# A softmax in four pieces between score tiles, and two fewer, larger weight and cache transfers, in a one-core decode block

## The chip, the cores and the metric

The kernel runs on one core of a Trainium2 chip. The metric is device microseconds (us) for one execution. Three executions took 187.05, 187.17 and 187.21 us, so the median is 187.17 us. One further execution was profiled; it took 187.01 us.

Engines are named as in the profile: PE is the matrix engine and PEld its weight load, DVE the vector engine, ACT the scalar engine, POOL the general engine, SP the engine that issues the DMAs. SPq is SP's instruction queue.

## What is computed

Two sequences with one new token each pass a transformer block: adaLN modulation, attention over a window of the cache, then a GELU-gated feed-forward part. Everything in memory is bf16.

```python
mod = (silu(c) @ w_mod)              # 640 -> 6*640: sa, ca, ga, sb, cb, gb
h = layernorm(x) * (1 + ca) + sa
q = (h @ wq)                          # 640 -> 32 heads * 192
k, v = k_cache[:, :, 3072:4096], v_cache[:, :, 3072:4096]   # W = 1024 keys
p = softmax(q . k * 192 ** -0.5)
x = x + ga * ((p . v) @ wo)           # 6144 -> 640
h = layernorm(x) * (1 + cb) + sb
x = x + gb * ((gelu(h @ w_gate) * (h @ w_up)) @ w_down)     # F = 1536
```

K and V of the window are 2 x 32 x 1024 x 192 values each, 25.2 MB each. With wq and wo (7.9 MB each), w_mod (4.9 MB) and the three feed-forward weights (2.0 MB each) one execution reads 76.9 MB.

## The kernel before

**The cache.** A partition holds a quarter of one head's window: 32 heads x 4 quarters = 128 partitions, 256 keys each. For each row b (0 or 1) these 256 keys are cut into four tiles of 64 (`NTL = 4`, `J = 64`), a tile is 3 MiB. Tiles lie in slots: slots 0 to 3 are the tensor `ring`, slots 4 and 5 the front of `r1` (shown as r), which holds wq first and wo last. `items` (L336) lists the cache loads in their order: tile pairs in one transfer of 6 MiB each, except V's last two tiles of row 1, which are two transfers of 3 MiB. I write K0a for row 0's tiles 0 and 1, K0b for its tiles 2 and 3, and V0a to V1b alike. `load_kv(n)` issues the items up to the n-th.

**The order.** A small scheduler (`_Sched`) keeps one list of operations for each engine, in the order in which the code calls `S.op` and `S.dma`; an engine works through its list in order and waits on semaphores for what it reads and overwrites. So where a call stands in the code sets its place in each queue. All DMAs are issued by SP, in the order: w_mod, c, x, wq, the cache items, wo, w_gate, w_up, w_down, out. A cache load waits until the last reader of its slots has ended: V0a for the K0b tiles' reductions, V0b for row 1's second tile, V1a for row 1's fourth tile, V1b for the two products of V0a (`PV0_0`, `PV0_1`). wo, which overwrites wq and slots 4 and 5, waits for `PV0_2` and `PV0_3`; the feed-forward weights wait for `PV1_0` and `PV1_1`.

**Scores.** `scores` (L554) goes through half tiles: `d_mul` (L465) multiplies half a K tile by q in place on DVE, `filler` gives PE four matmuls without a use (they hold its clock), `p_reduce` (L476) sums 12 slices on PE into a PSUM bank, and `d_rows` (L483) ends the sum of the half tile before on DVE.

**Softmax.** `softmax(b)` is a chain of nine short operations: `pmax` and `T` (maximum for each partition, then a PE transpose), `max`, `gx` and `Bc` (maximum for each head, scaled, then spread by a PE matmul), `nb` and `exp` (copy of the bias on DVE, exponential on ACT), `den` and `rden` (a PE matmul sums the denominators, DVE inverts). Both chains stand after the last score tile.

**Values.** `weighted` alternates `d_mask` (L511, DVE builds the masked probabilities `Em`, two buffers) and `p_pv` (L523, 32 matmuls on PE for one tile). `normalize` scales row 0's sums, then row 1's four tiles follow, then `p_sel` puts the heads in place and `oT` (L597) transposes in three parts.

**After attention.** wo comes in four transfers of 16, 16, 12 and 4 of its 48 tiles; the products are four groups on PE, each waiting for its transfer (L628). `warm(n, ...)` gives PE n idle matmuls after a group (`WO_WARM`). Then come the second layer norm, the gate product (L646, then 8 idle matmuls), the up product, the gate-up product on DVE (L660), a transpose, the down product in three parts (L669) and two DVE operations (L676, L678) before the output's DMA.

Of the kernel before, what the change touches and what calls it, by code (L numbers as in the profile page):

```python
# [5 lines left out]
ALU = mybir.AluOpType  # L6
ACTF = mybir.ActivationFunctionType
AX = mybir.AxisListType
# [95 lines left out]
def bass_adaLN_cond__sliding_block_cached__geglu_ffn__decode_kernel(  # L104
# [15 lines left out]
    P = 128  # L120
    B, _, D = A_x.shape
    _, H, Sk, Dh = A_k_cache.shape
# [13 lines left out]
    QP = P // H  # L136
# [10 lines left out]
    SCALE = float(Dh) ** -0.5  # L147
# [6 lines left out]
    NS = 4  # L154
    SL = J * Dh
    WQ_SPLIT = [5]
    assert sum(WQ_SPLIT) == KT
    WO_SPLIT = [16, 16, 12, 4]
    OT_SPLIT = [16, 16, 16]
    assert sum(WO_SPLIT) == NT and sum(OT_SPLIT) == NT  # L160
    WU_SPLIT = [5]
# [2 lines left out]
    assert sum(WD_SPLIT) == FT  # L164
    ND = 4

    WO_WARM = [0, 8, 0, 9]
    WU_WARM = [5]
    WD_WARM = [5, 0, 0]

# [1 line left out]
    with es:  # L172
        S = _Sched(nc, es)
# [38 lines left out]
        ident_f = sb("ident_f", [P, P], F32)  # L212
        one = sb("one", [1, 1], F32)
# [5 lines left out]
        DS = sb("DS", [P, P], F32)  # L219
# [16 lines left out]
        S_sb = Sg[:, :].rearrange("p (b k) -> p b k", b=2)  # L236
        gl = Sg[:, 0:FN]
        ones_f = Sg[:, 0:P]
        M1 = sb("M1", [P, 1], F32)
        gm = sb("gm", [1, H], F32)  # L240
        gx = sb("gx", [1, H, QP], F32)
        nb = sb("nb", [P, 1], F32)
        E_sb = sb("E_sb", [P, 2, KP], BF16)
        Em = sb("Em", [P, 2, J, H], BF16)
        esum = sb("esum", [P, 2], F32)
        rden = sb("rden", [P, 2], F32)
        On = sb("On", [P, 2, Dh], BF16)
        ps = es.enter_context(nc.psum_tensor("ps", [P, 8, 512], F32))

        BK_T = 2  # L250
# [8 lines left out]
        def bank(k):  # L259
            return ("bank", k)  # L260
# [6 lines left out]
        sem_wg = S.sem("d_wg")  # L267
        sem_wu = [S.sem("d_wu%d" % i) for i in range(len(WU_SPLIT))]
        sem_wd = [S.sem("d_wd%d" % i) for i in range(len(WD_SPLIT))]
        sem_ring = [S.sem("d_ring%d" % i) for i in range(4)]  # L270
        sem_out = S.sem("d_out")

        def k_dma(dst, src):
# [6 lines left out]
        def dram_rows(v):  # L280
# [9 lines left out]
             reads=[("S", 0, 0, 0), ("S", 0, 0, 1), ("S", 0, 1, 0), ("S", 0, 1, 1)], writes=["ident_f"], name="ident_f")  # L290
        S.op("pool", lambda e: e.tensor_copy(out=ident_b[:, :], in_=ident_f[:, :]),
             reads=["ident_f"], writes=["ident_b"], name="ident_b")
# [3 lines left out]
             reads=["ident_f"], writes=["G32"], name="G32")  # L296
        S.op("dve", lambda e: e.tensor_reduce(out=M32[:, :], in_=ident_f[:, :].rearrange("p (h t) -> p h t", t=QP), axis=AX.X, op=ALU.add),
             reads=["ident_f"], writes=["M32"], name="M32")
        S.op("dve", lambda e: e.tensor_copy(out=M32b[:, :], in_=M32[:, :]), reads=["M32"], writes=["M32b"], name="M32b")
        S.op("dve", lambda e: e.tensor_copy(out=Bsel[:, :].rearrange("p (a m) -> p a m", m=SQ),  # L300
                                            in_=G32[:, :].unsqueeze(1).broadcast_to([P, NJ, SQ])),
             reads=["G32"], writes=["Bsel"], name="Bsel")

        S.op("dve", lambda e: e.tensor_copy(out=DS[:, :].rearrange("p (a m) -> p a m", m=SQ),
                                            in_=M32[:, :].unsqueeze(1).broadcast_to([P, NJ, SQ])),
# [17 lines left out]
        def ring_keys(slot):  # L323
# [10 lines left out]


        items = [("k", 0, 0, 2, 0, 0), ("k", 0, 2, 2, 2, 1), ("k", 1, 0, 2, NS, 2), ("k", 1, 2, 2, 0, 0), ("v", 0, 0, 2, 2, 1),  # L336
                 ("v", 0, 2, 2, NS, 2), ("v", 1, 0, 2, 0, 0), ("v", 1, 2, 1, 2, 1), ("v", 1, 3, 1, 3, 3)]
        place = {(kind, b, t0 + i): slot + i for kind, b, t0, nt, slot, _ in items for i in range(nt)}
        assert NTL == 4 and len(place) == 4 * NTL

# [3 lines left out]
        def load_kv(upto, deps=()):  # L344
            while keep["kv"] < upto:
                kind, b, t0, nt, slot, sm = items[keep["kv"]]
                cache = A_v_cache if kind == "v" else A_k_cache
                S.dma("sp", k_dma(tile_f(slot, nt),
                                  cache[b, :, K0:Sk, :].rearrange("h (q r) d -> h q r d", q=QP)[:, :, J * t0:J * (t0 + nt), :].rearrange("h q r d -> h q (r d)")),
                      sem_ring[sm], writes=[k for i in range(nt) for k in ring_keys(slot + i)], deps=deps, name="ld_%s%d_%d" % (kind, b, t0))  # L350
                keep["kv"] += 1
# [108 lines left out]
        def filler(n=1):  # L460
            warm(n * ND, BK_W)
# [19 lines left out]
        def d_rows(b, t, hf):  # L481
            a = J * t + JH * hf
            S.op("dve", lambda e: e.tensor_reduce(out=S_sb[:, b, a:a + JH], in_=ps[:, hf, 0:JH * GC].rearrange("p (j c) -> p j c", j=JH),  # L483
                                                  axis=AX.X, op=ALU.add),
                 reads=[bank(hf)], writes=[("S", b, t, hf)], name="rows%d_%d_%d" % (b, t, hf))

        def softmax(b):
            sk = [("S", b, t, hf) for t in range(NTL) for hf in range(2)]
            S.op("dve", lambda e: e.tensor_reduce(out=M1[:, :], in_=S_sb[:, b, :], axis=AX.X, op=ALU.max),
                 reads=sk, writes=["M1"], name="pmax%d" % b)  # L490
            S.op("pe", lambda e: e.transpose(ps[0:1, BK_T, 0:P], M1[:, :], ident_f[:, :]),  # L491
                 reads=["M1", "ident_f"], writes=[bank(BK_T)], name="T%d" % b)
            S.op("dve", lambda e: e.tensor_reduce(out=gm[:, :], in_=ps[0:1, BK_T, 0:P].rearrange("k (h t) -> k h t", t=QP), axis=AX.X, op=ALU.max),
                 reads=[bank(BK_T)], writes=["gm"], name="max%d" % b)
            S.op("dve", lambda e: e.tensor_scalar(out=gx[:, :, :], in0=gm[:, :].unsqueeze(2).broadcast_to([1, H, QP]),
                                                  scalar1=-SCALE, scalar2=None, op0=ALU.mult),
                 reads=["gm"], writes=["gx"], name="gx%d" % b)
            S.op("pe", lambda e: e.matmul(ps[:, BK_T, P:P + 1], lhsT=gx[:, :, :].rearrange("k h t -> k (h t)"), rhs=one[:, :],  # L498
                                          start=True, stop=True),
                 reads=["gx", "one"], writes=[bank(BK_T)], name="Bc%d" % b)  # L500
            S.op("dve", lambda e: e.tensor_copy(out=nb[:, :], in_=ps[:, BK_T, P:P + 1]), reads=[bank(BK_T)], writes=["nb"], name="nb%d" % b)  # L501
            S.op("act", lambda e: e.activation(out=E_sb[:, b, :], in_=S_sb[:, b, :], func=ACTF.Exp, scale=SCALE, bias=nb[:, 0:1], accum_out=esum[:, b:b + 1]),  # L502
                 reads=sk + ["nb"], writes=[("E", b), ("esum", b)], name="exp%d" % b)
            S.op("pe", lambda e: e.matmul(ps[:, BK_T, P + 2:P + 3], lhsT=DS[:, :], rhs=esum[:, b:b + 1], start=True, stop=True),  # L504
                 reads=[("esum", b), "DS"], writes=[bank(BK_T)], name="den%d" % b)
            S.op("dve", lambda e: e.reciprocal(out=rden[:, b:b + 1], in_=ps[:, BK_T, P + 2:P + 3]),
                 reads=[bank(BK_T)], writes=[("rden", b)], name="rden%d" % b)


        def d_mask(b, t):  # L510
            S.op("dve", lambda e: e.tensor_tensor(out=Em[:, t % 2, :, :], in0=E_sb[:, b, J * t:J * (t + 1)].unsqueeze(2).broadcast_to([P, J, H]),  # L511
                                                  in1=M32b[:, :].unsqueeze(1).broadcast_to([P, J, H]), op=ALU.mult),
                 reads=[("E", b), "M32b"], writes=[("Em", t % 2)], name="mask%d_%d" % (b, t))

        def p_pv(b, t):
            vs = slot_of("v", b, t)
            n = J // 2

            def f(e):
                last = None  # L520
                for jp in range(n):
                    r = 2 * SQ * (jp % 2)
                    last = e.matmul(ps[r:r + 2 * H, BK_O, 0:ON],  # L523
                                    lhsT=Em[:, t % 2, 2 * jp:2 * jp + 2, :].rearrange("p j c -> p (j c)"),
                                    rhs=tile_v(vs)[:, 2 * jp:2 * jp + 2, :],
                                    start=(t == 0 and jp < 2), stop=(t == NTL - 1 and jp >= n - 2), tile_position=(0, r), skip_group_check=True)
                return last
            keep[("pv", b, t)] = S.op("pe", f, reads=[("Em", t % 2)] + ring_keys(vs), writes=[bank(BK_O)], name="PV%d_%d" % (b, t))
# [22 lines left out]
            S.op("pe", f, reads=["SEL"] + [("On", b, g) for g in range(NJ)], writes=[bank(BK_H + c) for c in range(NQC)], name="sel%d" % b)  # L551


        def scores(b, ta, tb):  # L554
            for t in range(ta, tb):
                for hf in range(2):
                    d_mul(b, t, hf)
                    filler()
                    p_reduce(b, t, hf)
                    if (b, t, hf) != (0, 0, 0):  # L560
                        d_rows(*((b, t, 0) if hf else (b, t - 1, 1) if t else (b - 1, NTL - 1, 1)))

        def weighted(b, ta, tb):
            for t in range(ta, tb):
                d_mask(b, t)
                p_pv(b, t)
# [2 lines left out]
        load_kv(4)  # L569
        scores(0, 2, 4)  # L570
        load_kv(5)
        scores(1, 0, 2)
        load_kv(6)
        scores(1, 2, 4)
        load_kv(7)
        d_rows(1, NTL - 1, 1)
        softmax(0)
        softmax(1)
        weighted(0, 0, 2)
        load_kv(9)  # L580
        weighted(0, 2, 4)
        normalize(0)
        for t in range(NTL):
            d_mask(1, t)
            p_pv(1, t)
            if t == NTL - 1:
                p_sel(0)
        normalize(1)
# [127 lines left out]
```

## Time and profile before

| what | value |
|---|---|
| median of three executions | 187.17 us |
| profiled execution, its own time | 187.01 us |
| its span, first to last instruction | 185.7 us |
| busy: PE, DVE, ACT | 117.2, 106.6, 13.9 us |
| DMA queue q1: data, share of 16 engines' span | 76.88 MB, 96.7% |
| mean granted PE clock | 0.915 |
| chain that ended last, by engine | DMA 43%, DVE 36%, PE 16% |

The chain that ended last is found backwards from the last instruction, from each step to what released it. It passes through several engines because transfers wait for buffers that the engines free. A transfer's time "to landing" runs from its issue to its completion, so it holds the time that it stood behind other transfers. Every landing time in the prediction is the issue plus that time, both from the DMA view, or the start of the instruction that waited for it.

### The profile page before, as it was taken

How to read it: one execution, taken by the hardware profiler on the slowest of the kernel's cores; microseconds unless marked ns; L12 is line 12 of the kernel's file. 1: busy time of each engine (PE TensorE's matmuls, PEld its weight loads, DVE VectorE, ACT ScalarE, POOL GpSimd, SP SyncE). 2: the span in 40 equal slices, each digit the busy share in tenths (PEclk: the TensorE clock that was granted, in tenths of full speed). 3: DMA queues.
4: the chain of work that ended last, by engine and by line, in shares of the span. 5: the costliest groups of instructions: out<-in, count | busy, mean ns of one | idle time of the engine just before them, and what ended most of it. 6: DMA issues, size and time to landing. Idle time of an engine off the chain costs nothing.

```text
span 185.7 us, 2254 instructions
## 1 busy us (share of the span) xinstructions
PE 117.2 (63%) x1014; PEld 60.8 (33%) x1014; DVE 106.6 (57%) x114; ACT 13.9 (7%) x24; POOL 4.9 (3%) x12
## 2 busy tenths in 40 slices
PE   0004500871079899988999885349928977299844
PEld 0001200440024334433344342226614654265422
DVE  6801600020598999999999993294556714803331
ACT  2001400013000000000000000200010004100400
POOL 8200000000000000000000000000000000000000
PEclk9999999998559999999999999558996999859999
DMA  7999998898999989899999989899999999999991
GB/s 248 414 437 477 463 463 389 371 491 371 487 413 434 468 381 459 381 487 402 455 424 434 459 381 466 381 487 413 395 434 424 424 435 424 413 408 435 422 392 50
DMA packets 2925, 77.02 MB, mean 415 GB/s; under 512 B 356, under 2 KB 356, under 8 KB 868
## 3 DMA queue, kind: packets, MB, share of 16 engines
q1 hardware_dynamic: 2916, 76.88, 96.7%
q8 instruction: 8, 0.13, 0.3%
q14 instruction: 1, 0.01, 0.0%
HBM read 76.88 MB, written 0.00 MB: 414 GB/s over the span
## 4 chain that ended last, share of the span: by engine, by line
DMA 43%; DVE 36%; PE 16%; SPq 1%; ACT 1%; issue 1%; POOL 1%; DVEq 0%; POOLq 0%
DMA ring<-in_A_k_cache_dram 24%; DVE ring L465 19%; DMA ring<-in_B_w_down_dram 18%; PE ps L523 10%; DVE r L465 7%; DVE Sg L483 5%; PE ps L476 4%; DVE Em L511 2%; SPq L274 1%; ACT E_sb L502 1%; PE ps L504 1%; PE ps L498 1%; DVE On L540 0%; ACT On L536 0%; PE ps L491 0%
## 5 line engine op out<-in xcount | busy, mean ns | idle before, releaser
L465 DVE TENSOR_TENSOR ring<-ring,qbc 128x6144 bf16<-128x6144 bf16 x12 | 40.1, 3351 | 8.4 <-DMA ring<-in_A_k_cache_dram 8.4
L476 PE MATMUL ps<-ring,ident_b 128*128 128x512 bf16 x144 | 34.7, 393 | 13.0 <-DVE ring L465 13.0
L454 PE MATMUL ps<-qbc,ident_b 128*128 128x384 bf16 x120 | 24.7, 339 | 0.7 <-ACT qbc L432 0.7
L523 PE MATMUL ps<-ring,Em 128*64 128x384 bf16 x192 | 19.6, 371 | 7.8 <-DVE Em L511 6.6
L476 PEld LDWEIGHTS ps<-ring,ident_b 128*128 128x128 bf16 x144 | 13.6, 100 | 32.7 <-DVE ring L465 17.2
L511 DVE TENSOR_TENSOR Em<-E_sb,M32b 128x2048 bf16<-128x2048 bf16 x8 | 18.1, 2288 | 5.5 <-PE ps L523 5.5
L523 PEld LDWEIGHTS ps<-ring,Em 128*64 128x64 bf16 x192 | 12.4, 125 | 14.6 <-DVE Em L511 7.3
L454 PEld LDWEIGHTS ps<-qbc,ident_b 128*128 128x128 bf16 x120 | 11.6, 101 | 10.9 <-issue 2.8
L401 PE MATMUL ps<-ring,scT 128*32 128x480 bf16 x40 | 4.4, 601 | 16.0 <-DVE scT L358 16.0
L465 DVE TENSOR_TENSOR r<-r,qbc 128x6144 bf16<-128x6144 bf16 x4 | 13.4, 3352 | 0.0
L483 DVE TENSOR_REDUCE Sg<-ps 128x32 f32<-128x512 f32 x16 | 11.0, 687 | 3.4 <-PE ps L476 3.4
L424 PE MATMUL ps<-r,hT 128*32 128x384 bf16 x80 | 5.8, 475 | 10.7 <-DMA r<-in_A_wq_dram 10.7
L476 PE MATMUL ps<-r,ident_b 128*128 128x512 bf16 x48 | 11.1, 380 | 1.8 <-DVE r L465 1.8
L434 DVE CAST aux<-ps 128x384 bf16<-128x384 f32 x4 | 2.0, 553 | 16.6 <-PE ps L424 15.7
L628 PE MATMUL ps<-r,aux 128*32 128x160 bf16 x192 | 5.1, 271 | 4.4 <-DMA r<-in_A_wo_dram 2.6
L424 PEld LDWEIGHTS ps<-r,hT 128*32 128x32 bf16 x80 | 3.2, 135 | 13.8 <-issue 11.6
L476 PEld LDWEIGHTS ps<-r,ident_b 128*128 128x128 bf16 x48 | 4.4, 98 | 8.1 <-DVE r L465 3.4
L401 PEld LDWEIGHTS ps<-ring,scT 128*32 128x32 bf16 x40 | 1.2, 132 | 17.5 <-DVE scT L358 16.0
L540 DVE TENSOR_SCALAR On<-ps,rden 32x192 bf16<-32x192 f32 x4 | 1.7, 418 | 8.9 <-ACT On L536 8.9
L502 ACT ACTIVATE E_sb<-Sg,nb 128x256 bf16<-128x256 f32 x2 | 1.0, 507 | 75.6 <-DVE nb L501 75.6
L628 PEld LDWEIGHTS ps<-r,aux 128*32 128x32 bf16 x192 | 4.3, 114 | 5.8 <-DMA r<-in_A_wo_dram 3.6
L523 PE MATMUL ps<-r,Em 128*64 128x384 bf16 x64 | 5.4, 327 | 0.0
(73 smaller groups left out, 65.6 us busy)
## 6 DMA issues: line engine op xcount, KB each, us to landing
ring<-in_A_k_cache_dram SPq DMA_DIRECT2D x3, 6144.0 KB, 40.3
ring<-in_A_v_cache_dram SPq DMA_DIRECT2D x2, 6144.0 KB, 23.3
r<-in_A_wq_dram SPq DMA_DIRECT2D x1, 7680.0 KB, 30.7
r<-in_A_k_cache_dram SPq DMA_DIRECT2D x1, 6144.0 KB, 38.4
r<-in_A_v_cache_dram SPq DMA_DIRECT2D x1, 6144.0 KB, 23.3
ring<-in_A_v_cache_dram SPq DMA_DIRECT2D x2, 3072.0 KB, 17.6
r<-in_A_wo_dram SPq DMA_DIRECT2D x2, 2560.0 KB, 23.7
ring<-in_w_mod_dram SPq DMA_DIRECT2D x1, 4800.0 KB, 14.2
```

The costliest lines, as they stand in the source:

```text
L274: return lambda e: e.dma_start(dst, src)
L401: last = e.matmul(ps[SQ * j:SQ * j + SQ, bk, 0:3 * DN].rearrange("p (i n) -> p i n", i=3), lhsT=scT[:, k, :], rhs=wm_v[:, k, 3 * part * D: ...
L424: last = e.matmul(ps[SQ * j:SQ * j + SQ, BK_H + c, 0:QC], lhsT=hT[:, k, :], rhs=wq_v[:, k, RN * j + QC * c:RN * j + QC * (c + 1)], start=( ...
L434: S.op("dve", lambda e: e.tensor_copy(out=dst, in_=src), reads=reads, writes=writes, name=name)
L454: last = e.matmul(ps[:, bk, 0:2 * Dh], lhsT=ident_b[:, :], rhs=qbc[:, :, :].rearrange("p b d -> p (b d)"), start=True, stop=True)
L465: S.op("dve", lambda e: e.tensor_tensor(out=tile_v(ks)[:, hf * JH:(hf + 1) * JH, :], in0=tile_v(ks)[:, hf * JH:(hf + 1) * JH, :], in1=qbc[ ...
L476: last = e.matmul(o_ap, lhsT=ident_b[:, :], rhs=tile_v(ks)[:, hf * JH:(hf + 1) * JH, ci * GC:(ci + 1) * GC], start=(ci == 0), stop=(ci == ...
L483: S.op("dve", lambda e: e.tensor_reduce(out=S_sb[:, b, a:a + JH], in_=ps[:, hf, 0:JH * GC].rearrange("p (j c) -> p j c", j=JH), axis=AX.X, ...
L502: S.op("act", lambda e: e.activation(out=E_sb[:, b, :], in_=S_sb[:, b, :], func=ACTF.Exp, scale=SCALE, bias=nb[:, 0:1], accum_out=esum[:, ...
L511: S.op("dve", lambda e: e.tensor_tensor(out=Em[:, t % 2, :, :], in0=E_sb[:, b, J * t:J * (t + 1)].unsqueeze(2).broadcast_to([P, J, H]), in ...
L523: last = e.matmul(ps[r:r + 2 * H, BK_O, 0:ON], lhsT=Em[:, t % 2, 2 * jp:2 * jp + 2, :].rearrange("p j c -> p (j c)"), rhs=tile_v(vs)[:, 2 ...
L628: last = e.matmul(ps[SQ * j:SQ * j + SQ, BK_M, 0:DN], lhsT=oT[:, t, :], rhs=wo_v[:, t, DN * j:DN * j + DN], start=(t == 0), stop=(t == NT ...
```

## The change

It has four parts.

1. `softmax` no longer issues its operations but returns four functions: `pmax` and `T`; `max`, `gx` and `Bc`; `nb` and `exp`; `den` and `rden`. `scores` takes such a list and calls one after each half tile. Row 0's four pieces now stand between the half tiles of row 1's tiles 0 and 1.
2. Row 1's four pieces are interleaved with row 0's first two masks and products.
3. V's last two tiles become one transfer of 6 MiB, issued after `PV0_1`, `den1` and `rden1` in the code; one DMA semaphore is dropped. After row 1's second value tile PE gets 20 idle matmuls (`filler(5)`).
4. wo comes in three transfers of 16 tiles, so its last group of matmuls is 64 long; before, groups of 48 and 16 ended it. The idle matmuls after the groups are 0, 8, 9; before they were 0, 8, 0, 9.

```diff
-    WO_SPLIT = [16, 16, 12, 4]
+    WO_SPLIT = [16, 16, 16]
-    WO_WARM = [0, 8, 0, 9]
+    WO_WARM = [0, 8, 9]
-        sem_ring = [S.sem("d_ring%d" % i) for i in range(4)]
+        sem_ring = [S.sem("d_ring%d" % i) for i in range(3)]
-                 ("v", 0, 2, 2, NS, 2), ("v", 1, 0, 2, 0, 0), ("v", 1, 2, 1, 2, 1), ("v", 1, 3, 1, 3, 3)]
+                 ("v", 0, 2, 2, NS, 2), ("v", 1, 0, 2, 0, 0), ("v", 1, 2, 2, 2, 1)]
...
+            def piece_max():      # pmax, T
+            def piece_head():     # max, gx, Bc
+            def piece_exp():      # nb, exp
+            def piece_den():      # den, rden
+            return [piece_max, piece_head, piece_exp, piece_den]
...
-        def scores(b, ta, tb):
+        def scores(b, ta, tb, pieces=()):
+            pieces = list(pieces)
             for t in range(ta, tb):
                 for hf in range(2):
                     d_mul(b, t, hf)
                     filler()
                     p_reduce(b, t, hf)
                     if (b, t, hf) != (0, 0, 0):
                         d_rows(*((b, t, 0) if hf else (b, t - 1, 1) if t else (b - 1, NTL - 1, 1)))
+                    if pieces:
+                        pieces.pop(0)()
...
-        scores(1, 0, 2)
+        scores(1, 0, 2, softmax(0))
...
         d_rows(1, NTL - 1, 1)
-        softmax(0)
-        softmax(1)
-        weighted(0, 0, 2)
-        load_kv(9)
+        pieces = softmax(1)
+        pieces[0]()
+        d_mask(0, 0)
+        pieces[1]()
+        p_pv(0, 0)
+        d_mask(0, 1)
+        pieces[2]()
+        p_pv(0, 1)
+        pieces[3]()
+        load_kv(8)
         weighted(0, 2, 4)
         normalize(0)
         for t in range(NTL):
             d_mask(1, t)
             p_pv(1, t)
+            if t == 1:
+                filler(5)
             if t == NTL - 1:
                 p_sel(0)
```

More of the change, by code (lines that the diff above doesn't have):

```diff
@@ L488, in softmax @@
             sk = [("S", b, t, hf) for t in range(NTL) for hf in range(2)]
[L489 to L505, printed above, removed]
@@ L506, in softmax @@
-            S.op("dve", lambda e: e.reciprocal(out=rden[:, b:b + 1], in_=ps[:, BK_T, P + 2:P + 3]),
-                 reads=[bank(BK_T)], writes=[("rden", b)], name="rden%d" % b)
+            def piece_max():
+                S.op("dve", lambda e: e.tensor_reduce(out=M1[:, :], in_=S_sb[:, b, :], axis=AX.X, op=ALU.max),
+                     reads=sk, writes=["M1"], name="pmax%d" % b)
+                S.op("pe", lambda e: e.transpose(ps[0:1, BK_T, 0:P], M1[:, :], ident_f[:, :]),
+                     reads=["M1", "ident_f"], writes=[bank(BK_T)], name="T%d" % b)
@@ new lines, in piece_head @@
+            def piece_head():
+                S.op("dve", lambda e: e.tensor_reduce(out=gm[:, :], in_=ps[0:1, BK_T, 0:P].rearrange("k (h t) -> k h t", t=QP), axis=AX.X, op=ALU.max),
+                     reads=[bank(BK_T)], writes=["gm"], name="max%d" % b)
+                S.op("dve", lambda e: e.tensor_scalar(out=gx[:, :, :], in0=gm[:, :].unsqueeze(2).broadcast_to([1, H, QP]),
+                                                      scalar1=-SCALE, scalar2=None, op0=ALU.mult),
+                     reads=["gm"], writes=["gx"], name="gx%d" % b)
+                S.op("pe", lambda e: e.matmul(ps[:, BK_T, P:P + 1], lhsT=gx[:, :, :].rearrange("k h t -> k (h t)"), rhs=one[:, :],
+                                              start=True, stop=True),
+                     reads=["gx", "one"], writes=[bank(BK_T)], name="Bc%d" % b)
@@ new lines, in piece_exp @@
+            def piece_exp():
+                S.op("dve", lambda e: e.tensor_copy(out=nb[:, :], in_=ps[:, BK_T, P:P + 1]), reads=[bank(BK_T)], writes=["nb"], name="nb%d" % b)
+                S.op("act", lambda e: e.activation(out=E_sb[:, b, :], in_=S_sb[:, b, :], func=ACTF.Exp, scale=SCALE, bias=nb[:, 0:1], accum_out=esum[:, b:b + 1]),
+                     reads=sk + ["nb"], writes=[("E", b), ("esum", b)], name="exp%d" % b)
+            def piece_den():
+                S.op("pe", lambda e: e.matmul(ps[:, BK_T, P + 2:P + 3], lhsT=DS[:, :], rhs=esum[:, b:b + 1], start=True, stop=True),
+                     reads=[("esum", b), "DS"], writes=[bank(BK_T)], name="den%d" % b)
+                S.op("dve", lambda e: e.reciprocal(out=rden[:, b:b + 1], in_=ps[:, BK_T, P + 2:P + 3]),
+                     reads=[bank(BK_T)], writes=[("rden", b)], name="rden%d" % b)
```

## The prediction

> **What bounds the kernel now.** I read the page's busy times and slices first, then the chain that ended last, then SP's timeline with each transfer's time to landing, then the timeline of the stretches that the change touches.
>
> ```profile
> PE 117.2 (63%) x1014; PEld 60.8 (33%) x1014; DVE 106.6 (57%) x114; ACT 13.9 (7%) x24; POOL 4.9 (3%) x12
> PEclk9999999998559999999999999558996999859999
> DMA  7999998898999989899999989899999999999991
> q1 hardware_dynamic: 2916, 76.88, 96.7%
> q8 instruction: 8, 0.13, 0.3%
> ```
>
> No engine is busy over 63%, while the DMA queue's packets fill 96.7% of 16 engines' span. The missing 3.3% is 6.1 us, and the two ends hold nearly all of it: the first 2 us and the 2.9 us after the last landing. So the span is about 2 us, then 76.88 MB without a hole, then a tail.
>
> ```profile
> 148.89 33.92 DMA ring<-in_B_w_down_dram
> 182.81 0.04 issue
> 182.85 0.35 PE ps L669 x8
> 183.20 0.02 issue
> 183.22 0.34 DVE lnt L676
> 183.56 0.02 issue
> 183.58 0.32 DVE sc L678
> ```
>
> This is the end of the chain. The last part of w_down lands at 182.81, having queued since 148.89. The tail behind it is eight matmuls, two DVE operations and the output's DMA, none of which the change touches. The end can move in two ways only: the stream ends at another time, or the compute before the tail becomes later than the stream.
>
> ```profile
> 82.59 0.54 SPq L274 DMA_DIRECT2D ring<-in_A_v_cache_dram  x1
> 98.05 0.54 SPq L274 DMA_DIRECT2D r<-in_A_v_cache_dram  x1
> 113.52 0.54 SPq L274 DMA_DIRECT2D ring<-in_A_v_cache_dram  x1
> ...
> 128.04 3.09 SPq L274 DMA_DIRECT2D ring<-in_A_v_cache_dram  x2
> 135.84 1.77 SPq L274 DMA_DIRECT2D r<-in_A_wo_dram  x4
> ```
>
> SP issues V0a, V0b and V1a at 82.59, 98.05 and 113.52, the two halves of V1b at 128.04 and 130.6. With 24.2, 23.3, 22.4, 15.2 and 20.1 us to landing they land at 106.8, 121.4, 135.9, 143.2 and 150.7. Each is issued 7.8 us or more before the one ahead of it has landed: that is the store of queued work that the change may use up.
>
> **Part 1, row 0's softmax between score tiles.** After K0a landed DVE runs without a gap, 3.27 + 0.60 us for each half tile, so what is inserted is paid in full: pmax 0.34, max and gx 0.51, nb 0.17. They wait for nothing: T and Bc stand on PE right behind a reduction that `rows` one half tile later has seen finished. The last piece does wait. den0 stands on PE behind the reduction of tile 1's second half, which starts when DVE's multiplication ends and takes 2.8 us; rden0 stands on DVE right after a `rows` of 0.6, and behind it the next multiplication. Reduction 2.8, den 0.4, rden 0.2, less the 0.6: DVE loses 2.8 us there. Together 3.8 us of delay at the end of the scores, 114.2 to 118.0. PE idles nearly 3 us meanwhile; if its clock halves, a reduction takes 4.34 instead of 2.76 (rows of L476) and DVE loses up to 0.6 more.
>
> Queued behind rden0 are all later multiplications, so the issues of V0b (+1.0, before rden0) and V1a (+3.8: 117.3). V0b, ahead of V1a, lands at 121.4. The output's 2.5 KB, issued at 183.93, shows 1.7 us from issue to landing; so V1a's data can flow from 119.0, 2.4 us before V0b has landed. The cover holds; gone, it would cost microsecond for microsecond.
>
> **Part 2, row 1's softmax among the masks.** From 113.5 to 121.2 the two chains ran one behind the other; only one is left, and a mask stands in its gap.
>
> ```profile
> 116.71 0.59 PE L504 MATMUL ps<-esum,DS 128*128 128x1 f32 x2 [0.89 <-ACT E_sb L502]
> 117.33 0.17 DVE L506 RECIPROCAL rden<-ps 128x1 f32<-128x1 f32 x1 [1.31 <-PE ps L504]
> ...
> 121.18 4.47 DVE L511 TENSOR_TENSOR Em<-E_sb,M32b 128x2048 bf16<-128x2048 bf16 x2
> 123.50 7.05 PE L523 MATMUL ps<-ring,Em 128*64 128x384 bf16 x64 [2.45 <-DVE Em L511]
> ```
>
> After 118.0: pmax 0.35, mask 2.3, max and gx 0.5, Bc 0.6, and the first products start at 121.9 (before 123.5). With 7.05 us for two tiles they end at 128.9, before 130.55. The merged V1b is issued then, 0.9 us later than the first half was and 1.7 earlier than the second; V1a, ahead of it, lands at 135.9. Hidden. But den1 and rden1 (0.8) now stand between `PV0_1` and the mask of tile 2 (2.3), which began at 128.07 before: tiles 2 and 3 run from 132 to 137.4 instead of 130.4 to 135.8 (5.4 us), or to about 138 if PE idling halved its clock. I take 138. wo is issued 2.2 us later, and 12 us of V1b still stand ahead of it.
>
> **Part 3, one transfer for V1b, 20 idle matmuls.** Normalise 1.8, mask 2.3, two products 7.1 (rows of 135.85 to 147.08): row 1's second tile ends at 149.2 instead of 147.1. The idle matmuls run at 0.18 each (nine took 1.64): 3.6 us, to 152.8. V1b is in by 150.6, so the idle matmuls, not the transfer, release the third tile. Two tiles of 2.6 end at 158.0, where the last one ended at 153.6: 4.4 us late. From there the steps are as before (selection, copies, three transposes of 1.4): wo's first group starts at 163.4 instead of 159.1, its second ends at 166.1, eight idle ones at 167.6.
>
> **Part 4, wo.** wo lands at 156.6, 162.7, 167.4 and 168.95 now. After it its third part of 16 lands at about 168.75, so the late products cost nothing by themselves: PE still waits. But 64 matmuls follow that landing (1.29 us in the row at 159.08) instead of 16 (0.46): they end at 170.1, not 169.5. All later steps keep their distance: the gate product ends at 175.7, its idle matmuls at 177.1. The up product cannot start before w_up has landed, 178.14 before; it showed 1.69 us of PE idle. The 0.6 fits.
>
> **The stream itself.** Equal bytes in fewer packets. The trace's DMA records give one packet 915.5 ns at 24 KB and 1818 at 48 KB: with eight for each engine and transfer, V1b saves 16 x 915.5 - 8 x 1818 = 104 ns. At 15, 5 and 20 KB they took 577, 198 and 765 ns: wo saves 8 x 10 = 80 ns. A completion packet takes 9 ns, and two go for each engine. Sum: 0.2 us. Landings bound it: V1b's halves took 14.8 us together, 6 MiB transfers 14.5 and 14.6; wo's last 16 tiles 6.2, the 16 before 6.1. So the gain is at most 0.4, at least 0; packets are the nearer row, I take 0.2.
>
> The Trainium skill, DMA: Bandwidth & Descriptors, section Measured, lists 1 MB at 341 GB/s and 16 MB at 425, and advises large batches. By it wo's 0.66 MB part would take at least 1.9 us, an estimate from that page, and merging it would save 0.3 more. Here it landed 1.57 us after its predecessor, 417 GB/s, because it queued behind other transfers; I take the trace.
>
> **Sum.** The stream ends 0.2 us earlier, the tail is unchanged, the compute delays lie beside it. The profiled execution goes from 187.01 to 186.8. The median shown is 0.16 above it, so 187.17 becomes 186.95. A change within 0.2%, 0.37 us, is about what a measurement of this kernel can't tell from none.
>
> **The rivals.**
>
> A, *compute passes the stream at wo* (slower). The budget: wo's last product may end 1.5 us later than before, at 170.9, before the up product is late; after it, 0.15 us more before the down product is. The place is the third group's clock.
>
> ```profile
> 157.60:161.00 3.40, 1.29 (x64) 1.12 (x64) 3.40 (x3) 0.93 (x1) 0.00 (x0) 1.00 0.97 416
> 161.05:164.45 3.40, 1.67 (x52) 1.67 (x56) 0.56 (x1) 0.00 (x0) 0.00 (x0) 0.50 1.02 428
> ```
>
> The columns are window, length, then busy time of PE, PEld, DVE, ACT, POOL, the granted clock, DMA share and GB/s. A window with 1.29 of 3.40 us of PE work was followed by half clock, at which 64 matmuls took 2.33 us. In the changed kernel the idle stretches near wo are 1.6 us (161.8 to 163.4) and 1.2 (167.6 to 168.8), over half busy in any such window; so I expect full clock. But if the products are done 1 us sooner, the second gap is 2.2 us. Then the group ends at 171.1, its nine idle matmuls take 3 us and hold the layer norm's statistics 2 us; the up product is 0.6 late, the end 0.3 to 0.5 later: 187.4. If the delay of 4.4 us grows beyond 6.3, or the gate product and its eight idle ones run at half clock too (2 us), 188 to 189.
>
> The Trainium skill, TensorE: Matmul & The Clock Gate, section on HAM oscillation, asks for no PE idle over about 3.4 us. Here 1.8 and 2.4 us, with few matmuls between, preceded half clock; by the page this rival would all but vanish, by the trace it stays.
>
> B, *each transfer costs more than its packets* (faster): the landings' bound of 0.4, or a little more: 186.7. Against it: the queue is full on both sides of both places.
>
> C, *instruction loads hit a lagging DMA engine*. Eight packets of 16 KB on q8 took 1.0 to 1.4 us each, and each held up one engine; the last engine sets a landing. The 20 idle matmuls bring 40 more PE instructions, so these loads come earlier. On an engine that lags already one costs up to 1 us: 187.7. For it the spread of w_down's end over the engines, about 2 us; against it, the engines held up before were all different.
>
> D, *V1a is issued too late*: the scores' end would have to slip more than 6.2 us, not 3.8. Then each further microsecond is one more: about 188.
>
> **How the numbers follow.** Forecast 0.55, A 0.2 (half of it still within 0.2%), B 0.14, C 0.07, D 0.04. Faster: B and a little of the forecast's spread, 0.2. Slower: half of A, C, D and some spread, 0.24. Same: 0.56. The range runs from below B, 186.5, to the first of A's larger cases, 187.9; the forecast's own is 186.75 to 187.2.
>
> **What would show it.** Right: no DMA slice falls below 9 after V1a's issue at about 117; DVE waits nearly 3 us for den0 once, near 97; V1b lands at 150.5; the third tile of row 1 waits for idle matmuls; the last part of w_down lands near 182.6 and is still the chain's last wait. Wrong: the chain passes through the up product's or the gate's predecessors on PE and DVE; half clock between 168 and 178; a hole in the DMA slices after 118; or w_down's landing moves by over 0.4 us.

## The result and the profile after

The changed kernel took 188.62 us (median of six executions, 188.08 to 189.14) against 187.11 us for the kernel before on the same chip: a ratio of the means of 1.0074, 95% interval 1.0051 to 1.0097. It is 0.74% slower. The prediction said 186.95 us, no measurable change, with a range up to 187.9. The profiled execution took 188.08 us, the shortest of the six; its span is 186.8 us, 1.1 more than before. So the profile can explain 1.1 us; what the other executions add to that, 0.5 us at the median, no profile shows.

The page of the changed kernel, its busy times, slices and main DMA queue:

```profile
PE 118.6 (64%) x1034; PEld 60.9 (33%) x1034; DVE 106.2 (57%) x114; ACT 13.9 (7%) x24; POOL 4.9 (3%) x12
...
PEclk9999999997558999999999999969798899999999
DMA  7999999899898989999898999989989899999991
...
q1 hardware_dynamic: 2628, 76.88, 96.3%
```

Equal bytes in 288 fewer packets, as computed; no engine became busier by more than the 20 idle matmuls. The slices of 4.7 us don't betray the loss: the one from 117 to 121 us, where V1a's data arrives, is an 8 before and a 9 after. The end of the chain that ended last:

```profile
152.22 31.75 DMA ring<-in_B_w_down_dram
183.97 0.04 issue
184.01 0.35 PE ps L691 x8
```

The last landing is still what ends last, with the same tail behind it; it has moved from 182.81 to 183.97. So the compute did not pass the stream in this execution. The stream itself lost time. SP's timeline, start and length of each issue:

```profile
84.05 0.54 SPq L274 DMA_DIRECT2D ring<-in_A_v_cache_dram  x1
100.47 0.54 SPq L274 DMA_DIRECT2D r<-in_A_v_cache_dram  x1
118.47 11.75 SPq L274 DMA_DIRECT2D ring<-in_A_v_cache_dram  x2
139.47 1.34 SPq L274 DMA_DIRECT2D r<-in_A_wo_dram  x3
```

V1a is issued at 118.47 instead of 113.52, 4.95 us later. Where the pieces stand, DVE's timeline shows one wait (in brackets) and a multiplication that starts behind it:

```profile
94.24 3.33 DVE L465 TENSOR_TENSOR r<-r,qbc 128x6144 bf16<-128x6144 bf16 x1
...
97.50 0.67 DVE L483 TENSOR_REDUCE Sg<-ps 128x32 f32<-128x512 f32 x1
...
100.55 0.17 DVE L515 RECIPROCAL rden<-ps 128x1 f32<-128x1 f32 x1 [2.37 <-PE ps L513]
100.64 3.34 DVE L465 TENSOR_TENSOR ring<-ring,qbc 128x6144 bf16<-128x6144 bf16 x1
```

From one multiplication to the next are 6.40 us here instead of 3.87. With 0.45, 0.45 and 0.06 for the three pieces before it the change delays DVE by 3.5 us. The other 1.46 us were there before the first piece: K0a landed 0.58 later (DVE began at 49.19, not 48.61), and the first reduction ran almost wholly at half clock (5.23 us at a granted clock of 0.52; before, 4.34 us at 0.63).

Now five microseconds around V1a's arrival. Columns: window, length, busy time of PE, PEld, DVE, ACT, POOL, granted clock, DMA share, GB/s. The kernel before:

```profile
117.00:122.00 5.00, 1.83 (x7) 1.28 (x6) 2.04 (x7) 0.60 (x2) 0.00 (x0) 0.50 1.09 472
```

The changed kernel:

```profile
117.00:122.00 5.00, 1.66 (x8) 0.51 (x6) 3.50 (x5) 0.00 (x0) 0.00 (x0) 1.00 0.92 334
```

A packet is counted where it starts, so a single window is coarse, but 472 against 334 GB/s is 0.7 MB. The DMA records say what happened. Each transfer ends on each of the 16 DMA engines with a completion packet of 4 bytes. V0b's stand from 119.0 to 121.3, 119.7 in the mean: on average an engine is done 1.6 us before the last one. V1a's first packets start at 119.8, 1.3 us after its issue. In the mean an engine stood idle for 0.49 us between 119 and 121; in the kernel before, not at all. And 13 packets behind the gap took over 2.4 us instead of 1.82; that is 0.69 us more for each engine. (The kernel's very first packets, of 38 KB, are slow too: 1.6 to 2.7 us, and 1.43 later.) Together 1.2 us.

### The profile page after: what moved, and what is told of

Its sections match the earlier page's. It is cut to its first block, busy times and chain, and to the rows that moved or that the text cites. A ratio compares the mean times of both kernels' runs of the same rounds, so it can differ in the third digit from the quotient of the medians.

```text
span 186.8 us, 2285 instructions
## 1 busy us (share of the span) xinstructions
PE 118.6 (64%) x1034; PEld 60.9 (33%) x1034; DVE 106.2 (57%) x114; ACT 13.9 (7%) x24; POOL 4.9 (3%) x12
## 4 chain that ended last, share of the span: by engine, by line
DMA 42%; DVE 36%; PE 18%; SPq 1%; issue 1%; POOL 1%; ACT 0%; DVEq 0%; POOLq 0%
DMA ring<-in_A_k_cache_dram 25%; DVE ring L465 19%; DMA ring<-in_B_w_down_dram 17%; PE ps L534 11%; DVE r L465 7%; PE ps L476 6%; DVE Sg L483 5%; DVE Em L522 4%; SPq L274 1%; DVE On L551 0%; ACT On L547 0%; DVE M L492 0%; PE ps L513 0%; DVE gx L500 0%; PE ps L503 0%
## 5 line engine op out<-in xcount | busy, mean ns | idle before, releaser
L476 PE MATMUL ps<-ring,ident_b 128*128 128x512 bf16 x144 | 35.6, 400 | 16.5 <-DVE ring L465 16.5
L454 PE MATMUL ps<-qbc,ident_b 128*128 128x384 bf16 x140 | 26.9, 326 | 0.7 <-ACT qbc L432 0.7
L534 PE MATMUL ps<-ring,Em 128*64 128x384 bf16 x192 | 19.1, 365 | 4.2 <-DVE Em L522 4.2
L454 PEld LDWEIGHTS ps<-qbc,ident_b 128*128 128x128 bf16 x140 | 13.1, 99 | 11.3 <-issue 2.3
L534 PEld LDWEIGHTS ps<-ring,Em 128*64 128x64 bf16 x192 | 11.8, 123 | 11.0 <-DVE Em L522 4.6
L424 PE MATMUL ps<-r,hT 128*32 128x384 bf16 x80 | 5.3, 447 | 11.3 <-DMA r<-in_A_wq_dram 11.3
L534 PE MATMUL ps<-r,Em 128*64 128x384 bf16 x64 | 7.1, 393 | 2.5 <-DVE Em L522 2.5
L650 PE MATMUL ps<-r,aux 128*32 128x160 bf16 x192 | 3.9, 233 | 3.5 <-DVE aux L619 1.8
L534 PEld LDWEIGHTS ps<-r,Em 128*64 128x64 bf16 x64 | 4.3, 131 | 5.0 <-DVE Em L522 2.5
```

The source lines that it names most:

```text
L424: last = e.matmul(ps[SQ * j:SQ * j + SQ, BK_H + c, 0:QC], lhsT=hT[:, k, :], rhs=wq_v[:, k, RN * j + QC * c:RN * j + QC * (c + 1)], start=( ...
L454: last = e.matmul(ps[:, bk, 0:2 * Dh], lhsT=ident_b[:, :], rhs=qbc[:, :, :].rearrange("p b d -> p (b d)"), start=True, stop=True)
L476: last = e.matmul(o_ap, lhsT=ident_b[:, :], rhs=tile_v(ks)[:, hf * JH:(hf + 1) * JH, ci * GC:(ci + 1) * GC], start=(ci == 0), stop=(ci == ...
L534: last = e.matmul(ps[r:r + 2 * H, BK_O, 0:ON], lhsT=Em[:, t % 2, 2 * jp:2 * jp + 2, :].rearrange("p j c -> p (j c)"), rhs=tile_v(vs)[:, 2 ...
L650: last = e.matmul(ps[SQ * j:SQ * j + SQ, BK_M, 0:DN], lhsT=oT[:, t, :], rhs=wo_v[:, t, DN * j:DN * j + DN], start=(t == 0), stop=(t == NT ...
```

## The experiments

The theory, formed from these traces, is the dry stream: V1a's late issue empties the engines, and the hole is never made up. Against it stood three rivals: instruction loads, late value products, and slower merged transfers. V1a's issue can be moved without touching the rivals' causes, and the other way round.

**The pieces taken out of the change.**

```diff
-        scores(1, 0, 2, softmax(0))
+        scores(1, 0, 2)
...
+        for piece in softmax(0):
+            piece()
         pieces = softmax(1)
```

> The changed kernel, but row 0's softmax stands whole behind the scores again, ahead of row 1's; the interleaved softmax of row 1, the merged V transfer, the 20 idle matmuls and wo in three parts stay. Theory (dry stream): the four pieces delay V1a's issue by 3.5 us, the DMA engines run out of V0b's packets before V1a's arrive, and that hole moves the end. Without the pieces V1a is issued near 113.5 to 115.0, no DMA slice near 119 falls, and the time is the kernel before's less the 0.2 us of packets: 186.9 (186.7 to 187.2). Rival 1 (instruction loads of 20 more idle matmuls hit a lagging DMA engine): nothing changes, 188.4. Rival 2 (the late value products make the compute pass the stream): the products are as late as in the changed kernel, 188.4 or more. Rival 3 (merged transfers move slower): 188.4.

186.92 us (186.71 to 188.45, twelve executions) against 187.07: 1.0001 (0.9986 to 1.0016). V1a is issued at 114.27. The loss is gone at the median with everything else of the change in place, so none of the three rivals carries it. Two of the twelve executions took 187.65 and 188.45 us, outside what was expected; their mean granted clock was 0.918, that of the other ten 0.925 to 0.936. No profile shows either of them, so their cause stays open. The window of the profiled execution (186.88 us) shows full flow:

```profile
117.00:122.00 5.00, 1.71 (x9) 1.18 (x11) 4.10 (x6) 0.40 (x2) 0.00 (x0) 0.61 1.09 472
```

**Only the wait taken out.** The last piece is cut in two, and `rden` goes behind the next half tile:

```diff
-            return [piece_max, piece_head, piece_exp, piece_den]
+            return [piece_max, piece_head, piece_exp, piece_den, piece_rden]
...
-        scores(1, 0, 2, softmax(0))
+        pieces0 = softmax(0)
+        scores(1, 0, 2, pieces0[:4])
...
-        scores(1, 2, 4)
+        scores(1, 2, 4, pieces0[4:])
...
+        pieces[4]()
```

> The changed kernel, but rden0 stands one half tile later on DVE than den0 is put on PE, so DVE does not wait for a reduction that has just begun; the same for nothing else. Theory (dry stream): the pieces now cost DVE 1.1 us instead of 3.5, V1a is issued 2.4 us earlier, before the first engine is out of packets, and the time is 186.9 (186.7 to 187.3), the same as with the softmax whole. Rivals 1, 2 and 3 (instruction loads, late compute, merged transfers): 188.4, no change, since their causes are all kept.

187.05 us against 187.07: 1.0014 (1.0000 to 1.0027). V1a is issued at 114.92 and no engine goes idle. So of the 3.5 us only the 2.5 us wait had to go. DVE's timeline, `rden` without a wait:

```profile
100.29 0.67 DVE L483 TENSOR_REDUCE Sg<-ps 128x32 f32<-128x512 f32 x1
100.89 0.14 DVE L517 RECIPROCAL rden<-ps 128x1 f32<-128x1 f32 x1
100.97 3.33 DVE L465 TENSOR_TENSOR ring<-ring,qbc 128x6144 bf16<-128x6144 bf16 x1
```

Four of the twelve executions took 187.7 to 187.9, which the theory did not foresee; they are taken up below.

**The pieces alone**, in the kernel before: `softmax` and `scores` as in the changed kernel, row 1's four pieces called in one go behind the scores, nothing else.

```diff
-        scores(1, 0, 2)
+        scores(1, 0, 2, softmax(0))
...
-        softmax(0)
-        softmax(1)
+        for piece in softmax(1):
+            piece()
```

> The kernel before with the first part of the change alone: row 0's softmax in four pieces between the half tiles of row 1's first two tiles; row 1's softmax whole behind the scores, V's last two tiles in two transfers, wo in four, no further idle matmuls. Theory (dry stream): the whole loss without the 0.2 us of packets, 188.2 to 189.2, spread over the executions as the changed kernel is. Rivals 1, 2 and 3: 187.1, as before, since none of their causes is in it.

188.28 us (187.91 to 189.07) against 187.07: 1.0071 (1.0053 to 1.0088). The first part alone makes the loss and its spread.

**A delay with no softmax in it**, in the kernel before:

```diff
         load_kv(6)
+        for _ in range(10):
+            S.op("dve", lambda e: e.tensor_reduce(out=scr[:, :], in_=S_sb[:, 0, :], axis=AX.X, op=ALU.max),
+                 reads=[("S", 0, t, hf) for t in range(NTL) for hf in range(2)], writes=["scr"], name="delay")
```

> The kernel before with ten reductions that nobody reads put on DVE ahead of the multiplication of row 1's third tile: 10 x 0.34 to 0.42 us, 3.4 to 4.2 us of delay for V1a's issue and nothing else of the change. Theory (dry stream): the same hole as in the changed kernel, 188.2 to 189.2, V1a issued at 117 to 119. If a late issue of V1a is covered, as the prediction had it: 187.1.

190.03 us, 1.0178 (1.0155 to 1.0202): more than expected. The ten reductions took 4.5 us, V1a was issued at 118.25, and the engines idled 0.48 us near 120 as foreseen. But they idled another 0.67 us near 136. This kernel still has both softmax chains behind its scores, and V1b's first half waits for the first product behind them, which here began at 127.9 instead of 123.5:

```profile
127.92 8.10 PE L524 MATMUL ps<-ring,Em 128*64 128x384 bf16 x64 [2.45 <-DVE Em L512]
```

The order of the changed kernel spares that second hole: it starts this product at 122.6 although its scores end 4.95 us later than before.

**More delay in the changed kernel**: five such reductions at the same place.

> The changed kernel with five reductions that nobody reads on DVE ahead of the multiplication of row 1's third tile: 2.25 us more delay (ten took 4.5). Theory (dry stream): V1a is issued 2.25 us later into engines that are dry already, so the loss grows one to one, 188.6 + 2.25 = 190.9. Any rival in which V1a's issue is covered: 188.6, unchanged.

191.54 us (190.37 to 192.55): 2.9 more than the changed kernel for an issue at 120.93, 2.5 us later. The profiled executions fit one to one: 190.37 against 188.08 us, 2.3 more. Two of the four executions stand near 190.5 and two near 192.5; what parts them no run shows. Its window:

```profile
117.00:122.00 5.00, 3.40 (x16) 1.27 (x14) 2.71 (x5) 0.00 (x0) 0.00 (x0) 1.00 0.43 187
```

**Without the 20 idle matmuls**, in the changed kernel:

```diff
             d_mask(1, t)
             p_pv(1, t)
-            if t == 1:
-                filler(5)
```

> The changed kernel without the 20 idle matmuls behind row 1's second value tile. Theory (dry stream): the hole at V1a is untouched, 188.3 to 188.9. Rival 1 (instruction loads, 40 PE instructions fewer): 187.0. Rival 2 (compute late at wo): the products end 2 to 3 us earlier, so 187.0 if lateness was the loss; with a longer idle stretch ahead of wo's last group its clock may halve, which would add up to 0.5.

188.45 us (188.15 to 188.53), 1.0072 (1.0059 to 1.0086): the loss stays, and the theory's time is met, but not by the hole alone. In this profile the hole is half as large, 0.6 us (V1a was issued at 117.93). Two other things stand beside it. After a 16 KB instruction packet of 0.94 us at 154.6 the completion packets of wo's first part are spread from 155.0 to 157.6, those of V1b just before only from 148.9 to 150.2; so later landings are late by their last engine. And wo's last group ran at half clock behind a longer idle stretch, so that here the compute ended last:

```profile
170.25 2.33 PE L648 MATMUL ps<-r,aux 128*32 128x160 bf16 x64 [3.40 <-DMA r<-in_A_wo_dram]
```

So this run by itself does not clear instruction loads or the clock of wo. That they are not the changed kernel's cause rests on the first and the third experiment: everything but the pieces, and no loss at the median; the pieces alone, without the 20 idle matmuls and the late products, and the whole loss.

All profiles together. The spacing is that of the engines' mean completion of V0b and of V1a, worked out from the DMA records; the median is that of all executions.

```
kernel                              delay of DVE  V1a issued  spacing  median
before                              0             113.52      14.60    187.1
pieces taken out                    0             114.27      14.54    186.92
rden later, 20 idle behind wo       1.0           114.66      14.59    186.91
rden later, wo in four              1.0           114.60      14.63    186.97
rden later                          1.0           114.92      14.60    187.05
without the 20 idle matmuls         3.5           117.93      15.19    188.45
before, ten reductions              4.5           118.25      15.69    190.03
pieces alone                        3.5           118.34      15.71    188.28
changed                             3.5           118.47      15.71    188.62
changed, five reductions            5.8           120.93      17.93    191.54
```

Up to 114.9 the issue costs nothing; from 117.9 on the spacing grows by 0.6, 1.1 and 3.3 us. Two medians hold more than that: the second hole with ten reductions, and the lag and half clock without the 20 idle matmuls. Nothing in between was run, so the point where the cover ends lies between. An estimate from the trace of before: its first engine is done with V0b at 118.9, less the 1.3 us from an issue to its first packet, is 117.6.

**The slower executions of the kernel with rden later.** In its profile (an execution of 186.88 us) the compute is the last wait, not the stream. PE's timeline around wo:

```profile
164.71 1.47 PE L454 MATMUL ps<-qbc,ident_b 128*128 128x384 bf16 x8
168.96 2.33 PE L654 MATMUL ps<-r,aux 128*32 128x160 bf16 x64 [2.78 <-DMA r<-in_A_wo_dram]
171.22 1.86 PE L454 MATMUL ps<-qbc,ident_b 128*128 128x384 bf16 x9
...
178.25 1.00 PE L672 MATMUL ps<-ring,hT 128*32 128x384 bf16 x20
```

Behind 2.78 us without work the 64 products of wo's third part took 2.33 us, half clock, and the up product at 178.25 follows the gate's idle matmuls without any wait for its weights: the slack is zero here. With the values done 2.3 us sooner than in the changed kernel, PE has more idle time ahead of wo's landing, 2.78 us instead of 1.66. Two kernels ask whether this makes the slower executions: one restores wo's four parts (`WO_SPLIT = [16, 16, 12, 4]`, `WO_WARM = [0, 8, 0, 9]`), one keeps three and fills the idle stretch (`WO_WARM = [0, 20, 9]`).

> The changed kernel with rden0 one half tile later than den0 and wo's four transfers of 16, 16, 12 and 4 with their idle matmuls restored. With three parts this kernel took 186.8 to 187.1 in most executions and 187.7 to 187.9 in four of twelve; its profile shows the last 64 products at half clock for 2.33 us behind 2.8 us of idle PE, and the up product without any wait for its weights. Theory (wo's late group): with 48 and 16 products in the last two groups the slower executions vanish, 186.9 to 187.2 throughout. Rival (the slower executions are V1a's hole, from a late first K tile): they stay, about one in three near 187.8.

> The changed kernel with rden0 one half tile later than den0 and 20 instead of 8 idle matmuls behind wo's second group, so PE is busy until just before wo's third part lands (168.4 against 168.9). Theory (wo's late group): full clock for the last 64 products, 1.29 us, and no slower executions: 186.8 to 187.1, median 186.9. Rival (the slower executions are V1a's hole): one in three near 187.8 stays.

With four parts: 186.97 us (186.77 to 187.11, eleven executions). With 20 idle matmuls: 186.91 us (186.75 to 187.04, eleven). No slower execution is left in either. That points to wo's late group; that its half clock made the slower executions is argued, since no profile shows one of them. The second one's PE timeline has full clock and slack again:

```profile
164.41 3.42 PE L454 MATMUL ps<-qbc,ident_b 128*128 128x384 bf16 x20
169.14 1.29 PE L654 MATMUL ps<-r,aux 128*32 128x160 bf16 x64 [1.31 <-DMA r<-in_A_wo_dram]
...
178.32 1.00 PE L672 MATMUL ps<-ring,hT 128*32 128x384 bf16 x20 [0.85 <-DMA ring<-in_B_w_up_dram]
```

Against 187.03 us for the kernel before both stand at 0.9994 (0.9985 to 1.0003 and 1.0002). They undo the loss; that they are faster than the kernel before is not shown.

## Why the prediction was wrong

The failed step is the cover of V1a's issue in part 1, put at 2.4 us, and with it rival D's threshold. In the changed kernel V1a's first packets started at 119.8, 0.8 us after the first engine had done V0b (119.0), and the hole cost 1.1 us.

**What bounds the kernel: right.** The chain still ends with w_down's landing and the unchanged tail, and the end moved as the stream's end did, by 1.16 us.

**The delay of DVE: right.** Forecast 3.8 us, 2.8 of it for rden0's wait; measured 3.5 and 2.5. The granted clock stayed at 1.00 there (97.2 to 100.6). The 4.34 us that the forecast took for a reduction at half clock were so in part only, as the granted 0.63 shows; it makes no difference to the sum.

**The cover: wrong, twice.** The prediction put V1a's first data at 119.0, "2.4 us before V0b has landed", and said "The cover holds". First, a landing is the last engine's end. In the trace of before, V0b lands at 121.4, but the first engine is done with it at 118.9. Against that the forecast's 119.0 is no cover at all; even with the 1.3 us from issue to first packet that the trace of after shows, for which 1.7 were taken, 0.3 us are left. Second, the forecast added its delay to an issue at 113.52, one execution's. In the profile with the pieces taken out it was 114.27, and in the changed kernel 1.46 us of its lateness came from K0a's landing and the clock. That alone is several times the 0.3 us.

**Rival D: right in kind, wrong in size.** It was given a chance of 0.04 and a threshold of 6.2 us of delay; the loss begins between 1.0 and 3.5 us. "Each further microsecond is one more" held: from 118.47 to 120.93 the spacing grew by 2.2 us. The first part of the loss is steeper, because the packets behind a gap are slow.

**Row 1's softmax among the masks: right.** Products began at 122.6 (forecast 121.9), V1b was issued at 129.7 and was in time, ahead of V1a's end. Tiles 2 and 3 ran from 132.4 to 139.4 (132 to 138). What the forecast did not name is the worth of this order: the delayed kernel before opened a second hole at V1b, this one did not.

**The idle matmuls and the late products: right.** The third value tile started behind the 20 idle matmuls, at 153.6 (152.8), the last ended at 158.9 (158.0). wo's third part was not held up.

**wo's longer last group: right.** It ran at full clock for 1.29 us, and the up product still waited 0.85 us for its weights.

**Rival A: right in mechanism, not the cause here.** Its condition, values done sooner and a gap ahead of wo, came true in the kernel with rden later: half clock behind 2.78 us of idle PE, slack zero, and executions 0.8 us slower that vanished with idle matmuls in the gap. It came true again without the 20 idle matmuls, with 3.40 us of idle PE. The prediction's estimate was 0.3 to 0.5 us of loss. The Trainium skill, TensorE: Matmul & The Clock Gate, section on HAM oscillation, names gaps of over about 3.4 us. Here 2.78 us were enough, as 1.8 and 2.4 with 1.29 us of work between them were in the kernel before; the measurement decides.

**The stream's gain of 0.2 us: neither shown nor refuted.** The kernels with all merged transfers and no hole stand up to 0.15 us below before at the median, within their intervals.

**Rival B: not seen.** No kernel was faster beyond its interval.

**Rival C: not the cause, but seen.** The pieces alone, without any further idle matmul, made the loss. In the profile without the 20 idle matmuls, though, an instruction packet did hold up an engine that set the later landings.

## What to carry to other kernels

Where a transfer's issue is delayed in a kernel bound by DMA, measure the cover from the issue plus the time to its first packet to the moment when the first engines finish the transfer ahead, not to that transfer's landing; and take the issue from several executions. A hole in a stream that is full to the end is paid in full (here 1.1 and 3.3 us of spacing moved the profiled time by 1.1 and 3.4), however idle the compute engines are. A wait put in between pieces of a pipelined loop costs the whole of the operation that it stands behind: the same small step one half tile later cost 0.1 us instead of 2.5.

## What was not expected of the hardware

Packets that restart an empty DMA queue are slow: 2.4 to 2.9 us for 48 KB instead of 1.82, so a hole cost 1.2 us for each engine where the idle time was 0.49. The 16 engines drift apart by 1.9 us (before) and 2.3 us (after) at V0b although each moves equal bytes. In the trace of before three engines end V0b at 120.7 to 120.9, all others by 120.2, and three 16 KB instruction packets of 1.0 us each had come by then. The records name no engine, but strung together from end to start they put those packets on these three, which stay late in the transfers that follow. That drift is what hid the thin cover.
